# Moving the row-sum check of a fused adaLN, attention and FFN kernel from behind its last matmul into its last FFN

## The chip, the cores and the metric

One core of a Trainium2 chip runs the program. The metric is the device time in microseconds of one execution; several executions are summed up by their median. A profile of one further execution shows what each engine did: TensorE (PE, with its weight loads as PEld), VectorE (DVE), ScalarE (ACT), GpSimd (POOL) and SyncE (SP, which here only issues transfers). A letter q behind an engine's name (PEldq, SPq) marks what its sequencer does itself: branches, waits, register loads, the issue of a DMA.

## The reference, cut to what matters

```python
x = A_x                                                  # (1, 2048, 448) bf16
sa, ca, ga, sb, cb, gb = (silu(c) @ w_mod) split in six  # vectors of 448
h = layernorm(x) * (1 + ca) + sa
x = x + ga * attention(h, A_wqkv, A_wo)   # 16 heads of 28; each query sees 8 keys: itself and
                                          # every second position back to 14
h = layernorm(x) * (1 + cb) + sb
x = x + gb * (silu(h @ B_w1) @ B_w2)      # 448 -> 1792 -> 448
return x
```

The softmax of the reference is the usual one, with the largest logit subtracted.

## The kernel before, in words

The 2048 tokens are held in four chunks (`NC = 4`) of four 128-row tiles each. `layer(...)` builds the whole layer; it is called twice. The first call builds the **fast program**, in which `p = exp(scale * logit)` is taken without subtracting a maximum. The second call builds the **safe program**, with the maximum, behind `with tc.If(bad > 0)` (L912). So the program ends in a branch: where every row sum of the fast program was usable, each of the five engines' instruction streams jumps over its part of the safe program (PE's part has 3,397 instructions, ahead of it lie 2,823 of the fast program).

Whether the sums were usable is found out in four steps at the end of `layer`:

- `sums_ok` (L868 to L876, DVE): the reciprocals `rc` of the row sums are compared with two limits and counted per partition into `cnt`.
- `sums_all` (L878 to L880, PE): one fp32 matmul with a column of ones adds the 128 counts into `ps_f`, a PSUM tile of one bank.
- `sums_bad` (L882 to L884, DVE): turns the sum into the integer `flag`, which is zero when all is well.
- `nc.values_load` (L889): each of the five engines reads `flag` into a register, a TENSOR_LOAD in each instruction stream. SP also does two checks of the register's range behind it.

The order of the instructions is written out by hand. Every piece of work is a `P.op(...)` with a number, and the string `ORDER` (L42 to L63) lists all 733 numbers in the order in which they are emitted; engines run their own share of it in that order. A DVE or PE piece that is emitted earlier stands earlier in that engine's stream, and nothing overtakes it.

The last part of `ORDER` is the second half of the FFN. `ffn1` makes the hidden activations (`ps_h`, L790, and the silu on ACT, L794). `ffn2` (L803) does, for each 128-row tile, 14 matmuls of 448 columns into a one-bank PSUM tile `ps_y` (L812), an add of `x_all` on DVE into an output tile `ot` (L817), and a store from SP (L820). Here `ps_y` and `ps_f` share one pool:

```python
one = ctx.enter_context(tc.tile_pool(name="one", bufs=2, space=PSUM))   # L228
```

It has two banks, and tiles take them in turn in the order in which they are allocated. The first matmul into a tile waits until the reader of the tile that had the bank before is done: with only `ps_y` tiles in the turn, that is the add of the tile before the last.

In the listing before, the numbers 730 (`sums_all`), 731 (`sums_bad`) and 732 (the load of the flag) stand behind the last FFN matmul and its add (718 and 719) and ahead of the last store (720). `sums_ok` (729) stands much earlier, and is done by 140.4 us.

Behind the branch lie, for all engines, a wait for the engine's own last work, on SP a wait for every outstanding store, and then two all-engine barriers (line L940 in the profile) with a clearing of the semaphores between them.

Of the kernel before, what the change touches and what calls it, by code (L numbers as in the profile page):

```python
# [62 lines left out]
)  # L63


# [151 lines left out]
def layer(ctx, tc, io, safe):  # L217
# [648 lines left out]
    bad = {}  # L866
# [18 lines left out]
    if not safe:  # L885
        ck = P.op(("dve", 1550.0), sums_ok, rc_done + wo_gated + w2_gated)
        cm = P.op(("pe", 200.0), sums_all, [ck] + misc_ready, take=("one",))
        cf = P.op(("dve", 80.0), sums_bad, [cm], give=((cm, "one"),))
        P.op(("pe", 100.0), lambda o: bad.update(v=nc.values_load(bad["flag"][:], min_val=0, max_val=128 * 2 * NB * H)), [cf] + f1_read[NC - 1][:1])  # L889
    P.emit("" if safe else ORDER)  # L890
    return bad.get("v")


@with_exitstack
def kernel(
    ctx: ExitStack,
    tc: tile.TileContext,
    A_x: bass.AP,
    A_wqkv: bass.AP,
    A_wo: bass.AP,  # L900
    B_x: bass.AP,
    B_w1: bass.AP,
    B_w2: bass.AP,
    c: bass.AP,
    w_mod: bass.AP,
    out: bass.AP,
):
    io = (A_x, A_wqkv, A_wo, B_w1, B_w2, c, w_mod, out)
    with ExitStack() as first:
        with tc.manual_schedule():  # L910
            bad = layer(first, tc, io, False)
    with tc.If(bad > 0):  # L912
        with ExitStack() as again:
            layer(again, tc, io, True)

# [29 lines left out]
```

## Time and profile before

| | us |
|---|---|
| Median of 3 runs | 183.14 (182.25 to 183.61) |
| Span of the profiled execution | 181.7 |
| PE busy in it | 168.4 (93%) |
| DVE, ACT, POOL busy | 104.1, 110.1, 25.8 |
| Last FFN matmul starts | 174.2 |
| Last add on DVE starts | 174.6 |
| Last store issued by SP | 176.2 |
| All engines through the last barrier | 181.7 |

The time is that of the whole execution as the device counts it, and the span runs from the first to the last instruction in the profiled execution, which is one execution of its own. The median lies 1.4 us above the span. PE is busy for 93% of the span, and the granted clock is at full speed until the last FFN matmul is done. The last 7 us have no PE work in them.

### The profile page before, as it was taken

To read this page: it belongs to the slowest core of one execution; us is meant where nothing else is said; L and a number is where in the kernel's file an instruction comes from. 1 tells how busy PE (TensorE), PEld (TensorE's weight loads), DVE (VectorE), ACT (ScalarE), POOL (GpSimd) and SP (SyncE) were. 2 spreads that over 40 slices of the span, in tenths; PEclk is the share of its full clock that TensorE was granted. 3 is DMA by queue.
4 is the path that set the end of the run, shared out by engine and by line. 5 is a ranking of instruction groups with operands and counts; after the bars stand their busy time and mean duration, and the time that the engine had idled before them with its cause. 6 is when DMAs were issued, how large, how long until landed. Compare 5 with 4: busy or idle time off the path is not lost.

```text
span 181.7 us, 3553 instructions
## 1 busy us (share of the span) xinstructions
PE 168.4 (93%) x1405; PEld 76.7 (42%) x1406; DVE 104.1 (57%) x219; ACT 110.1 (61%) x153; POOL 25.8 (14%) x86
## 2 busy tenths in 40 slices
PE   7999999888689999999999999999999999999940
PEld 2543333544245344334453455554443444435510
DVE  6699796899599988273459045984554020200410
ACT  2277949897589657779989569461794504244000
POOL 4656530000012220022000000032140000000000
PEclk9999999999999999999999999999999999999995
DMA  5993679949962223102200022134316000100211
GB/s 196 327 346 89 149 142 352 284 101 151 230 203 51 51 61 83 25 0 61 58 25 7 22 51 58 25 79 108 83 27 168 2 22 3 51 0 4 76 34 31
DMA packets 33343, 17.42 MB, mean 96 GB/s; under 512 B 24296, under 2 KB 32936, under 8 KB 33320
## 3 DMA queue, kind: packets, MB, share of 16 engines
q1 hardware_dynamic: 33168, 16.90, 36.1%
q8 instruction: 13, 0.21, 0.5%
q10 hardware_dynamic: 152, 0.23, 0.4%
q14 instruction: 10, 0.08, 0.2%
HBM read 9.12 MB, written 1.84 MB: 60 GB/s over the span
## 4 chain that ended last, share of the span: by engine, by line
PE 69%; DMA 12%; DVE 6%; ACT 6%; SPq 1%; POOL 1%; issue 1%; ACTq 0%
PE ps_h L790 25%; PE ps_y L812 24%; PE ps_wo L763 7%; DMA x_all<-in_A_x_dram 6%; PE ps_qk L619 5%; PE ps_v L643 4%; ACT p L679 4%; DMA oT<-o 3%; PE ps_o L729 2%; PE ps_l L671 2%; DMA wqk<-xn 2%; DMA w<-in_B_w_dram 1%; SPq L334 1%; DVE st L455 1%; POOL rs L472 1%
## 5 line engine op out<-in xcount | busy, mean ns | idle before, releaser
L790 PE MATMUL ps_h<-h,w 128*128 128x512 bf16 (+1 forms) x224 | 47.3, 380 | 0.0
L812 PE MATMUL ps_y<-w,both 128*128 128x448 bf16 x224 | 45.9, 353 | 0.0
L794 ACT ACTIVATE both<-ps_h 128x1024 bf16<-128x1024 f32 x28 | 28.0, 1022 | 25.2 <-PE ps_h L790 25.0
L679 ACT ACTIVATE p<-ps_l 128x896 bf16<-128x896 f32 (+1 forms) x36 | 30.7, 933 | 2.3 <-PE ps_l L671 2.1
L812 PEld LDWEIGHTS <-both 128*128 128x128 bf16 x224 | 20.8, 98 | 20.1 <-issue 1.1
L790 PEld LDWEIGHTS <-w 128*128 128x128 bf16 (+1 forms) x224 | 16.9, 96 | 27.0 <-issue 11.4
L817 DVE TENSOR_TENSOR ot<-ps_y,x_all 128x448 bf16<-128x448 f32 x16 | 9.9, 622 | 29.6 <-PE ps_y L812 29.2
L619 PE MATMUL ps_qk<-h,wp 128*128 128x512 bf16 (+1 forms) x96 | 20.0, 380 | 0.1
L703 DVE TENSOR_TENSOR p<-p,maskb 128x1792 bf16<-128x1792 bf16 (+1 forms) x18 | 19.5, 1099 | 0.5 <-ACT p L679 0.5
L465 ACT ACTIVATE screp<-x_all,mv 128x448 bf16<-128x448 bf16 x16 | 10.7, 666 | 9.9 <-POOL mv L462 9.5
L619 PEld LDWEIGHTS <-wp 128*128 128x128 bf16 (+1 forms) x128 | 9.3, 97 | 15.9 <-issue 6.1
L462 POOL TENSOR_SCALAR mv<-sums 128x2 f32<-128x2 f32 x10 | 3.4, 337 | 76.6 <-DVE x_all L766 76.6
L763 PE MATMUL ps_wo<-wo,oT 128*128 128x448 bf16 (+1 forms) x64 | 12.5, 353 | 1.8 <-DMA oT<-o 1.4
L766 DVE SCALAR_TENSOR_TENSOR x_all<-ps_wo,x_all 128x448 bf16<-128x448 f32 x16 | 9.5, 621 | 8.3 <-PE ps_wo L763 8.3
L485 DVE TENSOR_SCALAR xn<-x_all,mv,rs 128x512 bf16<-128x512 bf16 x23 | 8.9, 408 | 8.6 <-POOL rs L472 8.4
L643 PE MATMUL ps_v<-wv,h 128*128 128x448 bf16 (+1 forms) x56 | 11.1, 354 | 1.1 <-ACT p L679 0.7
L623 DVE CAST qk<-ps_qk 128x1024 bf16<-128x1024 f32 x10 | 12.0, 1215 | 0.0
L472 POOL TENSOR_TENSOR rs<-rs,negh 128x2 f32<-128x2 f32 x16 | 11.5, 717 | 1.3
L735 DVE TENSOR_TENSOR o<-ps_o,rc 112x448 bf16<-112x448 f32 (+1 forms) x18 | 11.2, 624 | 0.6
L729 PE MATMUL ps_o<-v,p 128*128 128x29 bf16 x288 | 9.6, 176 | 1.2 <-DVE gbc L438 0.6
L729 PEld LDWEIGHTS <-p 128*128 128x128 bf16 x288 | 8.8, 96 | 4.1 <-DVE p L703 0.9
L734 DVE RECIPROCAL rc<-ps_o 112x16 f32<-112x16 f32 (+1 forms) x18 | 4.5, 252 | 9.9 <-PE ps_o L729 9.9
(85 smaller groups left out, 148.4 us busy)
## 6 DMA issues: line engine op xcount, KB each, us to landing
out_dram<-ot SPq DMA_DIRECT2D x16, 112.0 KB, 1.8
both<-in_w_mod_dram SPq DMA_DIRECT2D x2, 672.0 KB, 5.7
x_all<-in_A_x_dram SPq DMA_DIRECT2D x3, 448.0 KB, 5.6
w<-in_B_w_dram SPq DMA_DIRECT2D x3, 448.0 KB, 6.2
w<-in_B_w_dram SPq DMA_DIRECT2D x1, 896.0 KB, 5.0
both<-in_w_mod_dram SPq DMA_DIRECT2D x2, 336.0 KB, 3.4
w<-in_B_w_dram SPq DMA_DIRECT2D x1, 672.0 KB, 5.5
wv<-in_A_wqkv_dram SPq DMA_DIRECT2D x2, 224.0 KB, 4.8
```

The costliest lines, as they stand in the source:

```text
L472: G.tensor_tensor(out=rs[:, j:j + n], in0=rs[:, j:j + n], in1=negh[:, 0:n], op=ALU.pow)
L619: T.matmul(ps[:, j, :], lhsT=w.rearrange("p h d -> p (h d)"), rhs=h[rows, :, t, 128:128 + CP], start=start, stop=stop)
L623: return [(either(act_ns(1024), dve_ns(1024)), lambda o, ps: copy_on(o)(out=qk[:, :, g, :, s0:s0 + CP], in_=ps[:].rearrange("p j (t s) -> ...
L643: T.matmul(ps[:, par, 0:D], lhsT=h[rows, par, t, b0:b0 + 128], rhs=wv[rows, t, :], start=(kk == ks[0]), stop=(kk == ks[-1]))
L679: S.activation(out=out_, in_=ps[:, :, 0:4 * nq].rearrange("p j (g q) -> p j g q", q=nq), func=ACTF.Exp, scale=SCALE)
L703: V.tensor_tensor(out=p, in0=p, in1=maskb[:, 1 if b == 0 else 0, 0:nq].unsqueeze(1).to_broadcast([128, H, nq]), op=ALU.mult)
L729: T.matmul(ps[:, h, 0:DH + 1], lhsT=p[:, at:at + 128], rhs=v[:, h, 0:DH + 1], start=True, stop=True)
L735: V.tensor_tensor(out=box["o"][0:nq, off:off + D].rearrange("p (h d) -> p h d", d=DH), in0=ps[0:nq, :, 0:DH], in1=r.unsqueeze(2).to_broadc ...
L763: T.matmul(ps[:, par, 0:D], lhsT=oT[rows, kk, par, s0:s0 + 128], rhs=wo[rows, par, kk, :], start=(q == qs[0]), stop=(q == qs[-1]))
L790: T.matmul(ps[:, j, :], lhsT=w, rhs=h[rows, :, t, :], start=start, stop=stop)
L794: return [(("act", act_ns(1024)), lambda o, ps: S.activation(out=hid[:, k % 2, :, i, :], in_=ps[:], func=ACTF.Silu), after + f2_read.get(k ...
L812: T.matmul(box["ps"][:, 0:D], lhsT=hid[:, k % 2, f % 2, f // 2, 128 * j:128 * j + 128], rhs=w2[:, f // 2 + 7 * (f % 2), :], start=(f == 0) ...
```

## The change

Two edits. In `ORDER`, 730 and 731 move from behind 719 to behind 656, and 732 moves to between 716 and 717. And the branch gets a label, with a hint given for it.

```diff
-    ... 650 651 654 655 656 631 687 638 639 640 641 "
+    ... 650 651 654 655 656 730 731 631 687 638 639 640 641 "
...
-    ... 722 723 724 725 715 716 717 718 726 706 707 727 728 719 730 731 732 720 721 "
+    ... 722 723 724 725 715 716 732 717 718 726 706 707 727 728 719 720 721 "
...
         P.op(("pe", 100.0), lambda o: bad.update(v=nc.values_load(bad["flag"][:], ...)), [cf] + f1_read[NC - 1][:1])
+        tc.mark_branch_hint_location("safe", "LikelyTaken")
...
-    with tc.If(bad > 0):
+    with tc.If(bad > 0, label="safe"):
```

What the two built programs hold, engine by engine:

- 656 is the add of tile 11's `ps_y`. Behind its last matmul PE now has the matmul of `ps_f`, and behind the add DVE has the making of `flag`. 631 is the first four matmuls of the next `ps_y` (tile 8). `ps_f` takes the turn in the two-bank pool that this `ps_y` had, and the built program shows it: its first matmul waited for the add of tile 10's `ps_y`, and now waits for the add of tile 11's, the one whose matmuls stand directly ahead.
- 715 to 718 are the 14 matmuls of the last tile, in groups of 4, 4, 4 and 2. PE's load of the flag now stands ahead of the last six of them, and nothing but these six stands between it and the branch.
- DVE's load stands ahead of the last two adds, SP's load and its two range checks ahead of the last three stores. ACT's and POOL's streams are unchanged: the load and the branch are the last things in both.
- The hint adds no instruction. The fast program has the same number of instructions on every engine in both builds (PE 2,823, DVE 246, ACT 172, SP 121, POOL 86), and no prefetch instruction is among them. The engines' branches carry the same fields as before.

4 rows, old and new, of the table ORDER are left out of this document.

## The prediction

> **What bounds the kernel now.** I read the chain of waits first, then the timeline of the last stretch, then the sequencers' rows of the branch, then the DMA queues. The chain says PE, up to the last add:
>
> ```profile
> PE 69%; DMA 12%; DVE 6%; ACT 6%; SPq 1%; POOL 1%; issue 1%; ACTq 0%
> ...
> 164.74 9.85 PE ps_y L812 x52
> 174.59 0.02 issue
> 174.61 0.62 DVE ot L817
> 175.24 0.05 DVE flag L884
> ```
>
> From 150 us to its last matmul PE works without a wait: what delays it there delays the last add one for one. But the chain stops at 175.3 us of 181.7. The timeline shows what follows:
>
> ```profile
> 174.50 0.19 PE L880 MATMUL ps_f<-onesf,cnt 128*1 128x1 f32 x2
> 174.61 0.62 DVE L817 TENSOR_TENSOR ot<-ps_y,x_all 128x448 bf16<-128x448 f32 x1 [2.02 <-PE ps_y L812]
> 175.15 0.14 DVE L884 TENSOR_SCALAR flag<-ps_f 1x1 int32<-1x1 f32 x1
> 176.22 0.33 SPq L820 DMA_DIRECT2D out_dram<-ot  x1
> ```
>
> The add ends at 175.24, and its store is issued at 176.22: SP reads the flag in between (478 ns), and checks its range. Then the rows of the loads and of the branch (mean ns; first and last start in us):
>
> ```profile
> L889 SPq TENSOR_LOAD <-flag x1: 478/478/478, 175.3 to 175.3; - x1
> L889 PEldq TENSOR_LOAD <-flag x1: 487/487/487, 175.3 to 175.3; - x1
> L889 DVEq TENSOR_LOAD <-flag x1: 545/545/545, 175.3 to 175.3; - x1
> ...
> L912 SPq EVENT_SEMAPHORE  x8: 17/17/17, 177.1 to 180.0; - x8
> L912 PEldq COMPARE_BRANCH  x1: 4298/4298/4298, 175.9 to 175.9; - x1
> L912 DVEq COMPARE_BRANCH  x1: 76/76/76, 175.9 to 175.9; - x1
> L912 DVEq EVENT_SEMAPHORE  x1: 21/21/21, 178.8 to 178.8; - x1
> L912 PEldq EVENT_SEMAPHORE  x1: 51/51/51, 180.3 to 180.3; - x1
> ```
>
> PE's jump over the safe program takes 4.30 us, to 180.2. SP's eighth wait, for the last store, ends at 180.0. Both then meet in the barriers. The two ends are one story: the DMA view shows instruction packets (q8, q14) in just this stretch, and the last store landing late, against the store issued at 148.75 in the second answer:
>
> ```profile
> q8 instruction: 2, 0.03, 2.1%
> q14 instruction: 4, 0.03, 1.8%
> ...
> out_dram<-ot SPq DMA_DIRECT2D x1, 112.0 KB, 3.8
> ...
> out_dram<-ot SPq DMA_DIRECT2D x1, 112.0 KB, 1.7
> ```
>
> Packet by packet: a 16 KB q8 packet runs from 177.73 to 178.76 on one DMA engine. The store's packets begin at 177.05; all but eight of its rows are through by 177.9, and these eight start at 178.76, as the q8 packet ends. q8 is PE's queue: its packets come once in about 256 PE instructions all through the run. So the fetch of PE's jump target both holds PE and holds back eight of the last store's 128 rows, which makes it land 2.1 us late.
>
> **The change, part by part.**
>
> *The wait put into PE, +0.87.* `ps_f` takes a turn in the two-bank pool, so the first matmul of tile 8 waits for the add of tile 11 instead of tile 10's.
>
> ```profile
> 147.51 2.44 PE L812 MATMUL ps_y<-w,both 128*128 128x448 bf16 x12
> 148.10 0.63 DVE L817 TENSOR_TENSOR ot<-ps_y,x_all 128x448 bf16<-128x448 f32 x1 [7.01 <-PE ps_y L812]
> 149.24 0.62 DVE L817 TENSOR_TENSOR ot<-ps_y,x_all 128x448 bf16<-128x448 f32 x1 [0.51 <-PE ps_y L812]
> ```
>
> The twelve matmuls, one each 0.189 us, are two of tile 10, six of tile 11, four of tile 8; tile 8's first starts at 147.51 + 8 x 0.189 = 149.03. Tile 11's add ends at 149.86; with 0.04 from DVE to another queue (the flag ends at 175.29, the loads start at 175.32 to 175.33) the matmul starts at 149.90. Queued behind it is all of PE's work, with ACT's silu and DVE's adds behind that. No wait follows on PE that would take it up. The `ps_f` matmuls (0.19 us) lie inside this wait: nothing. `flag` (0.14 us) follows the add on a DVE that idles: nothing. Last matmul, last add: 0.87 later.
>
> *PE's load of the flag, 0.* It holds PE's sequencer for 0.49, with the step to the next instruction 0.59 (175.33 to 175.92). TensorE notices only if the sequencer is less far ahead of the array. [...] If instead the load stops the array, it costs up to 0.59 plus 0.42 (the longest refill that PEld shows as issue time): 1.0.
>
> *PE's branch, off the path.* Nothing behind the load stops the sequencer. [...] Without any lead it starts at 175.4, when the last matmul ends.
>
> [...]
>
> *SP's load leaves the path, -0.96.* The store follows its add as the other stores do, 0.03 behind its end (168.80 to 168.83), instead of 0.98. It is issued at 176.22 + 0.87 - 0.96 = 176.13. On SP the load and checks now stand ahead of three stores; the first goes out some 0.5 us later, and no add waits for its buffer. DVE's load (0.55) fits in the 2.02 us that DVE idles before its next add.
>
> *The last store's landing, -1.98.* [...] The landing is the common 1.8 (median of 16) instead of 3.78; DVE's own fetch may still brush it, which is why I don't take 1.66, the quickest.
>
> *What follows, 0.* From the last landing (180.02 on SP) to the end 1.69, as before. [...]
>
> *The hint, 0.* It put no instruction into any stream.
>
> Sum: 0.87 - 0.96 - 1.98 = -2.07; the span goes from 181.70 to 179.6. The median lies 1.44 above the span, which I keep: 181.1.
>
> [...]
>
> **The rivals.**
>
> *The branch comes late (22%).* The branch, or its fetch, is held until the array is done with the last matmul, 174.57 + 0.87 = 175.44. Then PE's packet runs from 177.26 to 178.28, again across the store. Before, SP's end came 2.94 behind the q8 packet's: 181.22, 0.48 below before, 182.7. For it: the old branch was taken on an idle array, so no row shows one taken ahead. [...]
>
> *The load half counts (12%).* The array idles for about 0.6 at the load, the rest holds: 181.7.
>
> *Slower: the load drains PE (5%).* The load waits until the array is empty and the branch until the last matmul is done. PE then loses 1.0 more, the last matmul ends at 176.44, q8's packet ends 2.84 later at 179.28, the end is 182.22, +0.5: 183.7. It decides from a lead under 0.1, where 0.87 + 1.0 exceed what the earlier branch gives. [...]
>
> *The change doesn't do what it says (3% beyond the above).* For the hint this holds already. Were it live, PE's target would come sooner, and SP would still end at 179.6.
>
> **How the numbers follow.** My forecast has 58%: 181.1, its own range 180.5 to 181.7 with the spread of the runs shown (0.4%). The range for 8 in 10 reaches to the late branch: 180.5 to 182.9. A measurement of this kernel can tell about 1% (1.83 us) from no change; 181.3 is that mark, near the forecast. Three quarters of its chance (0.44) and 0.03 from the half-priced load and the live hint make 0.47 faster; slower by over 1% needs more than the draining alone: 0.05; the rest, 0.48, is within 1%.
>
> **What would show it.** Right: a PE wait of about 0.9 us on DVE at 149 us in front of L812; last add at 175.5; last store 0.03 behind its add's end, landing in 1.7 to 1.9; PEldq's COMPARE_BRANCH starting before the last matmul. Wrong: an idle array behind PE's TENSOR_LOAD; a branch that starts at 175.4 or later; a landing over 3 us. No wait at 149 us would make the sum wrong by 0.87.

## The result and the profile after

The changed kernel takes 181.89 us (median of 20 runs, 181.0 to 182.53), the kernel before 182.76 on the same chip (20 runs, 181.86 to 183.61). The ratio is 0.9951, with a 95% interval of 0.9935 to 0.9967: 0.9 us faster, half a per cent. A second measurement gave 0.9963 (0.9946 to 0.9979). The profiled execution of the changed kernel has a span of 179.6 us and a time of 181.66.

The end of the changed kernel's chain of waits, from 160 us on:

```profile
6 pieces in order of time: start us, us, what
...
165.10 9.85 PE ps_y L812 x52
174.96 0.02 issue
174.98 0.62 DVE ot L817
```

PE is still the chain up to the last add, which now ends at 175.60 and has no `flag` behind it. The price of that stands 25 us earlier, in the timeline around 149 us, and in the page's group of these matmuls:

```profile
147.00 1.69 PE L812 MATMUL ps_y<-w,both 128*128 128x448 bf16 x8
...
148.62 0.19 PE L880 MATMUL ps_f<-onesf,cnt 128*1 128x1 f32 x2
148.73 0.62 DVE L817 TENSOR_TENSOR ot<-ps_y,x_all 128x448 bf16<-128x448 f32 x1 [0.51 <-PE ps_y L812]
149.27 0.14 DVE L884 TENSOR_SCALAR flag<-ps_f 1x1 int32<-1x1 f32 x1
149.41 0.92 PE L812 MATMUL ps_y<-w,both 128*128 128x448 bf16 x4 [0.60 <-DVE flag L884]
```
```profile
L812 PE MATMUL ps_y<-w,both 128*128 128x448 bf16 x224 | 46.1, 353 | 0.6 <-DVE flag L884 0.6
```

The eight matmuls of tiles 10 and 11 run without a gap, then PE stands for 0.60 us until tile 11's add has ended. The view names `flag` as the releaser, but `flag` ends only as the matmul starts, at 149.41, and its semaphore counts 0.01 behind that start. The add ends at 149.35, and its semaphore counts 0.04 ahead of the matmul. From the first of the eight to the first of the next four it is 2.41 us, where it was 8 x 0.189 = 1.51.

The last stretch in the timeline, and the sequencers' rows of the loads and branches (mean ns; first and last start in us):

```profile
174.21 0.73 PE L812 MATMUL ps_y<-w,both 128*128 128x448 bf16 x3
174.98 0.62 DVE L817 TENSOR_TENSOR ot<-ps_y,x_all 128x448 bf16<-128x448 f32 x1 [2.02 <-PE ps_y L812]
175.63 0.33 SPq L820 DMA_DIRECT2D out_dram<-ot  x1
```
```profile
L889 DVEq TENSOR_LOAD <-flag x1: 689/689/689, 169.7 to 169.7; - x1
L889 SPq TENSOR_LOAD <-flag x1: 491/491/491, 170.1 to 170.1; - x1
L889 PEldq TENSOR_LOAD <-flag x1: 493/493/493, 170.4 to 170.4; - x1
```
```profile
L913 SPq EVENT_SEMAPHORE  x8: 17/17/17, 176.6 to 177.9; - x8
...
L913 PEldq COMPARE_BRANCH  x1: 3475/3475/3475, 171.4 to 171.4; - x1
L913 PEldq EVENT_SEMAPHORE  x1: 51/51/51, 175.0 to 175.0; - x1
L913 DVEq COMPARE_BRANCH  x1: 76/76/76, 175.0 to 175.0; - x1
...
L913 DVEq EVENT_SEMAPHORE  x1: 21/21/21, 177.9 to 177.9; - x1
```

The store goes out 0.03 behind its add. PE's branch (its jump over the safe program) starts 3.2 us ahead of the last matmul and is over at 174.87, 0.7 before the last add ends. SP's eighth wait, for the last store, ends at 177.9, and so does DVE's jump. The DMA view of 175.45 us to the end has both kinds of instruction packets in it still, and the **landing** of the last store (the time from its issue until SP's wait for it starts to run) is 2.2 us and not the common 1.7:

```profile
q14 instruction: 4, 0.03, 1.9%
q8 instruction: 1, 0.02, 1.1%
...
out_dram<-ot SPq DMA_DIRECT2D x1, 112.0 KB, 2.2
```

Single profiles reach this part of the last FFN at different times (tile 10's last two matmuls at 147.51 before, at 147.00 after), so I compare below the **stretch** from there to the end of the span: 34.19 us before, 32.55 after.

### The profile page after: what moved, and what is told of

The parts are those of the page before. It is cut to its first block, busy times and chain, and to the rows that moved or that the text cites. A ratio compares the mean times of both kernels' runs of the same rounds, so it can differ in the third digit from the quotient of the medians.

```text
span 179.6 us, 3554 instructions
## 1 busy us (share of the span) xinstructions
PE 168.7 (94%) x1406; PEld 76.7 (43%) x1406; DVE 103.9 (58%) x219; ACT 110.1 (61%) x153; POOL 26.1 (15%) x86
## 4 chain that ended last, share of the span: by engine, by line
PE 70%; DVE 10%; DMA 7%; ACT 6%; POOL 3%; issue 2%; SPq 0%; ACTq 0%; DVEq 0%
PE ps_h L790 25%; PE ps_y L812 24%; PE ps_wo L763 7%; PE ps_qk L619 5%; PE ps_v L643 4%; ACT p L679 2%; PE ps_o L729 2%; DMA oT<-o 2%; DMA x_all<-in_A_x_dram 2%; DVE p L703 2%; DVE st L455 2%; PE ps_l L671 2%; ACT xn L483 2%; DMA wqk<-xn 2%; DMA h<-xn 2%
## 5 line engine op out<-in xcount | busy, mean ns | idle before, releaser
L643 PE MATMUL ps_v<-wv,h 128*128 128x448 bf16 (+1 forms) x56 | 11.1, 354 | 1.0 <-ACT p L679 0.7
L542 DVE TENSOR_SCALAR h<-h,modc 128x512 bf16<-128x512 bf16 x15 | 5.6, 407 | 8.6 <-DMA h<-xn 8.6
```

Source lines behind the costliest of these rows:

```text
L643: T.matmul(ps[:, par, 0:D], lhsT=h[rows, par, t, b0:b0 + 128], rhs=wv[rows, t, :], start=(kk == ks[0]), stop=(kk == ks[-1]))
```

## The experiments

**The kernel before, once more.** No edit.

> The kernel before, unchanged, profiled once more. Theory A (PE's instruction fetch collides with the last store in the ordinary execution): the last store lands over 3 us after its issue again, PE's COMPARE_BRANCH takes about 4.3 us again, and the span is within 0.5 us of 181.7. Theory B (the profiled execution of before was an unlucky one, and the ordinary one has no collision or a shorter one): the landing is 1.7 to 2.5 us, or PE's branch about 3.5 us as in the changed kernel, and the span is 180.3 to 181.0. Time ratio to before 1.000 within 0.002 under both.

Measured: 1.000 (0.998 to 1.002), span 181.0, PE's jump 4.30, landing 3.76, stretch 34.16. The collision at the end is ordinary in this kernel, as theory A had it. The span is 0.7 under the first profile's, more than theory A's 0.5, and the difference stands ahead of the end: tile 10's last two matmuls are at 146.83 here, 0.7 earlier.

**The load alone behind the last store.**

```diff
-    ... 728 719 730 731 732 720 721 "
+    ... 728 719 730 731 720 732 721 "
```

> Before, with the flag's load (732) put behind the last store (720): SP issues the store 0.03 us behind its add, and PE loads and branches as before. Theory A (the jump of PE, 4.3 us from 175.9, sets the end by itself and through the packet that holds back the store): the end moves by 0 to 0.25 us, ratio 0.9985 to 1.000. Theory C (what counts is that SP's load stands in front of the last store): 0.96 us less, ratio 0.9948, as much as the whole change gave.

Measured: 0.9996 (0.9981 to 1.001). The store goes out 0.03 behind its add and lands in the common time, and nothing is won. The DMA view from 174.5 us and the branch's rows of this kernel:

```profile
q8 instruction: 2, 0.03, 2.9%
...
out_dram<-ot SPq DMA_DIRECT2D x1, 112.0 KB, 1.7
```
```profile
L912 SPq EVENT_SEMAPHORE  x8: 17/17/17, 176.6 to 177.2; - x8
...
L912 PEldq COMPARE_BRANCH  x1: 3878/3878/3878, 175.5 to 175.5; - x1
...
L912 PEldq EVENT_SEMAPHORE  x1: 51/51/51, 179.4 to 179.4; - x1
```

SP is done by 177.2, and PE comes in at 179.4. SP's load in front of the store counts for nothing while PE's jump is behind the last matmul: the two ends of the kernel before have to move together.

**The sum and `flag` early, the load where it was.**

```diff
-    ... 654 655 656 631 687 ... 728 719 730 731 732 720 721 "
+    ... 654 655 656 730 731 631 687 ... 728 719 732 720 721 "
```

> Only 730 and 731 moved, as in the change; the load of the flag (732) stays in front of the last store and behind all matmuls. The flag is ready 25 us before it is read, so SP reads it while it waits for the add, and PE's sequencer reaches the load ahead of the array. Theory A: PE's branch starts 1 to 2 us before the last matmul here too, the store is issued 0.03 us behind its add, the bank wait of 0.89 us is there; DVE reads the flag behind its last add and branches 0.6 us later than in the changed kernel. Ratio 0.995 to 0.998. Theory D (the load inside the matmuls is what lets PE branch early): PE's branch starts at 175.5 or later, and the ratio is 1.000 or above.

Measured: 0.9987 (0.9964 to 1.001), which overlaps the expectation at its upper edge only and does not settle the time. The trace settles the branch: PE's starts at 172.0, 2.6 us ahead of the last matmul, so no position of the load is needed for that, only a `flag` that is ready. Its first q8 packet is over by 174.0. But the store lands late all the same:

```profile
q14 instruction: 3, 0.02, 1.8%
q8 instruction: 1, 0.02, 1.1%
...
out_dram<-ot SPq DMA_DIRECT2D x1, 112.0 KB, 3.3
```

The q8 packet in this view is a second one, from 176.83 to 177.79. PE has entered the target by 175.5 and its queue fetches another 16 KB; the store's packets begin at 176.46, straight before it. So this order pays the bank wait and still collides: of theory A the early branch and the early store came true, and the ratio did not.

**The change without the turn in the pool.** The sum goes into column 448 of tile 11's own `ps_y` bank (its add reads columns 0 to 447), and no tile `ps_f` is allocated. `y_box[11]` holds that tile for the purpose; the lines that fill it, that drop the turn in the pool and that let `flag` read the new place are left out below. All else is as in the changed kernel.

```diff
-    ... 655 656 730 731 631 687 ...
+    ... 655 730 656 731 631 687 ...
...
-        bad["ps"] = onet("ps_f")
-        T.matmul(bad["ps"][0:1, 0:1], lhsT=bad["n"][:], rhs=onesf[:], start=True, stop=True)
+        bad["ps"] = y_box[11]["ps"][0:1, D:D + 1]
+        T.matmul(bad["ps"], lhsT=bad["n"][:], rhs=onesf[:], start=True, stop=True)
```

> The changed kernel, but the check's matmul writes a spare column (448) of tile 11's ps_y and takes no turn in the two-bank pool; it stands behind that tile's last matmul, ahead of the add. Theory A: the wait of 0.6 us on DVE in front of L812 at 149 us is gone, the last add comes 0.85 us earlier, and so does the end: ratio to before 0.990 to 0.991 against 0.995 for the change. Theory E (the lost time is taken up by slack further on): the ratio stays at 0.995.

Measured: 0.9911 (0.9888 to 0.9933), 181.25 us: faster than the kernel before by 1.6 us and than the changed kernel by some 0.7. The two intervals against the kernel before do not meet. Its timeline shows the wait gone:

```profile
147.51 1.69 PE L812 MATMUL ps_y<-w,both 128*128 128x448 bf16 x8
...
149.13 0.19 PE L880 MATMUL ps_y<-onesf,cnt 128*1 128x1 f32 x2
...
149.25 0.93 PE L812 MATMUL ps_y<-w,both 128*128 128x448 bf16 x4
149.36 0.62 DVE L817 TENSOR_TENSOR ot<-ps_y,x_all 128x448 bf16<-128x448 f32 x1 [0.63 <-PE ps_y L880]
```

From the eight matmuls to the next four it is 1.74 us, against 2.41 with the wait and 1.51 before; the 0.23 left over is about the sum's own matmul (0.19). The stretch is 31.86, 0.69 under the changed kernel's. This version beats both kernels.

**Both kernels without a far jump.** The safe program behind the branch is cut to one 16-byte transfer, so the target lies close behind the branch.

```diff
...
-        with ExitStack() as again:
-            layer(again, tc, io, True)
+        tc.nc.sync.dma_start(out=out.flatten_outer_dims()[0:1, 0:8], in_=A_x.flatten_outer_dims()[0:1, 0:8])
```

> Before, with the safe program behind the branch cut to one transfer of 16 bytes. The safe program is left out; for these inputs it is never run, and the branch is taken as before. Theory A (the far jump is the cost: it holds PE, and its instruction packet holds back the last store): PE's branch takes under 1 us, the last store lands in 1.7 to 2.0 us instead of 3.8, and the time falls by 1.5 to 2.0 us, ratio 0.989 to 0.992. Theory C (the load ahead of the store and the barriers are the cost): ratio 0.998 to 1.000.

> The changed kernel with the safe program cut in the same way. Theory A: where no far jump is left to hide, the change has only SP's load to give (0.96 us) and the bank wait to pay (0.89 us), so this kernel is level with the other short one within 0.3 us: ratio to before 0.989 to 0.992. Theory F (the change gives its 0.9 us whatever the jump costs): 0.9 us below the other short one, ratio 0.984 to 0.987.

Measured against the kernel before, on one chip: 0.9902 (0.9876 to 0.9928) for the kernel before so cut, 0.9887 (0.9866 to 0.9908) for the changed one. They are level with each other within their intervals. The second lies just under theory A's range, and its interval reaches into theory F's; what speaks against F is the other cut kernel, only 0.2 us slower beside it (180.97 and 180.79). PE's branch in the first of them, and the DMA view of the same kind of stretch in the second (all its rows of queues):

```profile
L912 PEldq COMPARE_BRANCH  x1: 223/223/223, 175.6 to 175.6; - x1
```
```profile
q1 hardware_dynamic: 144, 0.11, 6.1%
...
out_dram<-ot SPq DMA_DIRECT2D x1, 112.0 KB, 1.7
```

There is no q8 and no q14 packet in it, and the landing is 1.67 in both. So leaving the far jump out is worth 1.8 us to the kernel before (0.0098 x 182.8) and still 1.2 to the changed one (181.97 measured beside it, 180.79 cut): the change takes only a part of it away. The cut changes more than the distance, though. SP now runs its branch ahead of the last store (at 175.59, its range checks from 175.9, the store at 176.24 in the first; at 173.93 in the second), so in the first the store goes out 1.29 us behind its add instead of 0.98, and in the second 0.03. Without a far jump the change brings 0.3 us or nothing: the earlier store, worth 1.26 here, against the bank wait of 0.9.

**A hint that is in the program.** The kernel before, with the hint given for all engines; then it is an instruction, and the builder puts it at the head of each stream.

```diff
+        tc.mark_branch_hint_location("safe", "LikelyTaken", engines=mybir.ALL_ENGINES)
-    with tc.If(bad > 0):
+    with tc.If(bad > 0, label="safe"):
```

> Before, with the hint given for all five engines by name, so that each stream holds one prefetch instruction; the builder puts it at the head of the program, 175 us ahead of the branch. Theory G (what is fetched at the head is long replaced by the program's own blocks when the branch comes): PE's branch takes 3.9 to 4.3 us still, ratio 0.999 to 1.001. Theory H (the hint holds until the branch): PE's branch under 1 us, landing under 2 us, ratio 0.989 to 0.992.

Measured: 1.0017 (1.0001 to 1.0034). Neither theory holds whole. The time shows no gain, as theory G had it, yet the rows of the hint and of the branch show that the hint works, as theory H had it:

```profile
L941 PEldq BRANCH_PREFETCH_HINT  x1: 50/50/50, 0.9 to 0.9; - x1
```
```profile
L913 SPq EVENT_SEMAPHORE  x8: 17/17/17, 176.9 to 179.6; - x8
...
L913 PEldq COMPARE_BRANCH  x1: 393/393/393, 175.7 to 175.7; - x1
...
L913 PEldq EVENT_SEMAPHORE  x1: 51/51/51, 176.1 to 176.1; - x1
...
L913 DVEq EVENT_SEMAPHORE  x1: 21/21/21, 176.3 to 176.3; - x1
```

PE's jump takes 0.39 us instead of 4.30, DVE is through at 176.3, and all engines but SP are at the barrier by 176.5. SP's eighth wait ends at 179.6 all the same. The DMA view says why:

```profile
q14 instruction: 4, 0.03, 2.9%
q8 instruction: 1, 0.02, 1.3%
...
out_dram<-ot SPq DMA_DIRECT2D x1, 112.0 KB, 3.5
```

PE runs on at 176.14 and has one q8 packet behind its branch instead of two, from 176.81. That is 0.72 us behind the end of PE's branch, where the second packet stands in most of the other profiles (0.73 to 0.75), so it is not the one that a jump waits for. With three q14 packets from 176.73, 176.78 and 176.91 it lies on the store's packets, which begin at 176.83. The hint takes away the wait of the jump, but not the other packets. With `load_last` this is the other half of one finding: there the store was early and PE late, here PE is early and the store late, and neither alone moves the end. (The cut kernel before shows that a short jump helps without an earlier store when no packets come with it.)

**The changed kernel, once more.** No edit.

> The changed kernel, unchanged, profiled once more. If the changed kernel's first profile was an ordinary execution: landing of the last store 1.7 to 2.3 us, the stretch from tile 11's first matmuls (147 us) to the end 32.5 us. If it was a lucky one: a landing of 2.5 to 3.3 us, by a second instruction packet of PE that follows the jump's target, and 0.5 to 1.0 us more in that stretch. Ratio to before 0.994 to 0.997 under both.

Measured: 0.9963 (0.9946 to 0.9979). Its profile is of a long execution (183.24 us, the longest of its ten; those two matmuls start only at 148.39), and its stretch is 32.74, with a landing of 2.42. Both lie between the two cases of the expectation, nearer to the ordinary one.

**Three more profiles of the kernel before, one of the changed one.** No edits. The question was why the profiles differ by 1.5 us behind the last matmuls and the medians by 0.9.

> An unchanged copy of the kernel before, for one more profile. Two profiles of it had 34.19 and 34.16 us from tile 10's last two matmuls to the end of the span, the changed kernel 32.55 and 32.74: 1.5 less, where the medians differ by 0.9. Theory V (the stretch behind the last matmul varies): PE's jump, 4.30 in both profiles, and the landing, 3.78 and 3.76, are not always so long; this profile has a jump of 3.5 to 4.2 and a stretch of 33.4 to 34.0. Theory H (the stretch is fixed, the work ahead of it varies): jump 4.3, landing 3.8, stretch 34.1 to 34.2, and the start of these two matmuls moves between 146.3 and 147.5.

> A second unchanged copy of the kernel before, read as the one ahead of it: by theory V at least one of the three copies has a stretch under 33.9 us, by theory H all three lie within 0.1 of 34.17.

> A third unchanged copy of the kernel before: as for the second.

> An unchanged copy of the changed kernel, for one more profile. By both theories the stretch is 32.5 to 32.8 us, as in two profiles. PE's second q8 packet starts 0.9 to 1.0 us behind the start of the last matmul and the store's packets 1.87 behind it in both of them; if that is the order of the instructions and not chance, it is so here too, and the last store lands in 2.2 to 2.4 us and not in 1.8.

Measured, with the two earlier profiles of each (us):

| | before (five) | after (three) |
|---|---|---|
| start of tile 10's last two matmuls | 147.51, 146.83, 146.75, 147.54, 147.53 | 147.00, 148.39, 147.29 |
| PE's jump | 4.30, 4.30, 3.98, 4.18, 4.10 | 3.48, 3.38, 3.40 |
| landing of the last store | 3.80, 3.76, 3.49, 3.71, 3.60 | 2.23, 2.42, 2.27 |
| stretch | 34.19, 34.16, 33.89, 34.10, 34.00 | 32.55, 32.74, 32.58 |

Jump and landing vary, as theory V had it, but only just by its measure (one copy of 33.89), and the start varies by more. Theory H, with a fixed stretch, falls by two copies (33.89 and 34.00). The mean stretches differ by 1.45 us (34.07 and 32.62), the mean spans by 1.1 (181.30 and 180.18). The timed executions have spans on record too, 65 of the kernel before and 31 of the changed one in all runs here: their means differ by 1.08 us (180.89 and 179.81) and their mean times by 0.92. So the traced spans differ no more than the timed ones. Of the 1.45, 0.33 goes because tile 10's last two matmuls start later in the changed kernel's profiles (147.56 in the mean, 147.23 before), and 0.16 lies outside the span: the time is 1.97 us above the span before and 2.13 after (medians). Whether the starts differ by chance, with three to five profiles of each, stays open.

In all three profiles of the changed kernel PE's second q8 packet starts 0.9 to 1.0 us behind the start of the last matmul and the store's packets 1.87 behind it. So the overlap belongs to this order of instructions and is no accident of one profile.

## Why the prediction was right, and where not

The forecast was 181.1; 181.89 lies in its range and 0.8 above it. It was 183.14 (the median then known) less 2.07. Of the difference, 0.38 is the median, 182.76 over more runs, downwards, and 1.2 the sum, -0.9 measured instead of -2.07, upwards. So a part of the closeness is luck: two errors of opposite sign. The 1.2 can be laid out with the means above: the landing gained 0.6 less than forecast, which leaves -1.45 for the stretch; the later starts leave -1.12 for the traced spans; 0.16 outside the span, and 0.04 between traced and timed spans, leave -0.92.

- *The wait put into PE, +0.87.* Right: the last matmul starts 27.59 us behind tile 10's last two, before 26.71: +0.88. `no_turn` shows that it is the loss: with the wait gone the time falls by 0.7 us. Right in its cause too: the matmul starts 0.05 behind the end of tile 11's add. That `ps_f` and `flag` cost nothing beside it held.
- *PE's load, 0.* Right. Behind it the timeline has one row of 27 matmuls in 5.27 us (26 x 0.189 + 0.35), no gap. How far PE's sequencer is ahead of its array no row of before shows, so the 0 was the author's estimate; here it is seen: the branch starts 3.2 us ahead of the last matmul's start, with 17 matmuls and 16 weight loads still to begin. (In the rival of a load that stops the array, 0.42 is not PEld's longest issue time; one of 1.0 stands at L643. The rival did not happen.)
- *PE's branch, off the path.* Right: 171.4, the target reached 0.7 ahead of the last add's end. The first q8 packet runs from 172.42 to 173.45, 1.03 to 2.06 behind the branch, where before it was 1.8 to 2.8. The rival of a late branch and that of a draining load fall with it.
- *SP's load leaves the path, -0.96.* Right: from the last add's start to the store's issue 0.65 instead of 1.61.
- *The last store's landing, -1.98.* This is the term of the sum that was mis-sized. The landing fell from 3.80 to 2.23, -1.57 in these two profiles and -1.37 in the means of the table. The step counted one q8 packet for the jump and took it to be out of the way, which no row of before shows; it was, by 173.45. It left out that a second 16 KB packet of PE's queue follows once PE is in the target (here 0.73 us behind the end of its branch). Before, that one came at 181.26, behind everything, as the kernel before's DMA view of 181 to 182 us shows:

```profile
DMA packets 1, 0.02 MB, mean 16 GB/s; under 512 B 0, under 2 KB 0, under 8 KB 0
...
q8 instruction: 1, 0.02, 6.0%
```

Moving the branch 4.5 us earlier moved it to 175.60 to 176.61, onto the first packets of the store (from 176.46), with a q14 packet, 1.08 us behind SP's branch, in the tail of it. Without any instruction packet near it the store lands in 1.67 (`short_before`, `short_after`) or 1.7 (`load_last`). Of the 0.56 above that, 0.32 lies between the store's first and last packet (0.79 us against 0.47), and 0.24 behind the last one, where the q14 packet runs (177.10 to 177.56). No run takes away only one of the two. The trace of before had this second packet in plain sight; the branch took both its packets along.

- *What follows, 0.* Right: 1.69 from SP's last wait to the end in both. The cut kernels and the hinted one have 1.29 and 1.38 there: two steps of POOL in the last barrier lie 0.08 apart in them and 0.39 here. No run shows what makes that difference.
- *The hint, 0.* Right for this change. That a live hint would leave SP's end where it was, at the store's landing, was right as well for the kernel before.
- *The median, 1.44 above the span.* Wrong: the median of three executions was set against the span of one of them. An execution's time lies 1.88 to 2.06 above its own span in the kernel before and 2.06 to 2.21 in the changed one (1.7 to 1.8 in the cut ones, so the distance is not even a constant). The profiled execution of before, 181.70, was by this the 183.61 among the three runs, the slowest; the mean of all spans on record is 180.89. The span of 179.6 was met to 0.1 by luck: a slow base and too large a gain cancelled.

What the jump costs is measured; why it costs that is not. PE's branch takes 0.22 us with a near target (`short_before`, `short_after`), 3.4 to 3.5 with a far one where it starts ahead of the last matmul (the changed kernel, `flag_early`, `no_turn`), 3.9 in `load_last`, where two q14 packets run beside its first q8 packet, and 4.0 to 4.3 in the kernel before, where the store's packets run there as well. With a far jump and no hint two q8 packets come, with the hint one (176.81), with a near target none. No run shows what they hold, nor how a hint given at 0.9 us still shortens a jump at 175.7.

## What to carry to other kernels

Where a kernel ends in several chains that meet in a barrier, price the end only for all of them moved together: the early store alone gave 0.9996, the hinted jump alone 1.0017, early store and early jump together 0.9951 and, without the wait for a bank, 0.9911. A small tile that takes a turn in a rotating pool can make its neighbour wait for one more reader, here for 0.7 us; a spare column of a tile that is read anyway cost only its own instruction here (0.19 us). And a base for a forecast needs a profile whose own time is known to be ordinary, or several.

## What the runs showed of the hardware

- The far jump of this kernel costs PE 3.4 to 4.3 us and DVE 2.9 to 3.2 (ACT and SP 0.4 to 0.5 in the kernel before), and with it come two 16 KB packets of PE's queue: one that starts 1.0 to 1.8 us behind the branch and is over before the jump is (by 1.46 us in the first profile of before, by 1.42 in that of the changed kernel), and one 3.1 to 3.9 us after the first. A store that met such packets landed later: in 2.2 to 2.4 us with an overlap at the store's start, in 3.3 to 3.8 with one in its middle or with several fetches at once, against 1.67 alone. In the five profiles of before and in `flag_early` the store's last eight rows start within 0.02 us of the end of the q8 packet.
- A branch hint at the head of the program (at 0.9 us in `hint_live`) still made PE's jump short 175 us later (0.39 us for 4.30); the kernel before has eleven q8 packets in front of that branch.
- Not tried: the hint together with the version without the turn. An estimate from the rows of both: PE's one packet 1.1 us behind its branch, at 172.4, clear of the store, so up to 0.5 us of landing (2.19 there, 1.67 alone); DVE's packet would still be near the store.
